# The second MLP of an attention-and-two-MLPs kernel: five pairs of 436-column halves in place of four pairs of 512 and a plain state block

## The chip, the cores and the metric

The kernel runs on one core of one Trainium2 chip. The metric is device time in microseconds (us) of that core, from launch to end, as the median of several runs. The core has a matrix engine (TensorE, PE in the profile, with its weight loads shown apart as PEld), two elementwise engines that matter here (VectorE, DVE, and ScalarE, ACT), and a queue processor (SyncE, SP) that issues every DMA of this kernel in one order.

## The reference, cut to what matters

```python
def _attn_ref(x, state):                      # x (8, 8, 512, 64), state (8, 8, 32, 64)
    scores = scale * np.matmul(x, state.transpose(0, 1, 3, 2))      # softmax over the 32 states
    ...
    xread = np.matmul(a, state)
    ...
    sread = np.matmul(a2, x)
    return np.concatenate([xread, sread], axis=2)

def _moe_ref(x, w_in, w_out):                 # x (4352, 512), w_in (512, 2048), w_out (2048, 512)
    h = x @ w_in
    r = np.maximum(h, 0.0)
    return (r * r) @ w_out

def _moe2_ref(x, w_in, w_out):                # the second MLP: ELU in place of the squared ReLU
    h = x @ w_in
    g = np.where(h > 0.0, h, alpha * (np.exp(np.minimum(h, 0.0)) - 1.0))
    return g @ w_out
```

Each of the 8 batches gives 512 token rows and 32 state rows, so both MLPs see 8 x 544 = 4352 rows. Everything is float32 in effect: a product is made from a high and a low part of each operand in three passes (`product`, lines 41 to 45), low x high, high x high and high x low.

## The kernel before

The data lie transposed, with features on the 128 partitions and tokens along the columns, so a matmul moves up to 512 token columns past a 128x128 block of weights.

**First MLP** (to about 655 us). Attention, the conversion of the 64-bit weights, the first MLP on the eight batches of 512 columns, and at its end the first MLP on the 256 state columns (8 x 32). The conversion also writes, for later, the sums of weight quarters that the second MLP needs (`sums`, `put_split`: DRAM tiles `f_w2..` and `f_v2..`, seven forms of 256 columns with a high and a low part, 2 KB a row and form) and the plain weights `d_w2..`, `d_v2..`. What the first MLP computes is stored into the DRAM tiles `x2d`, one for each batch and one for the state rows.

**Second MLP** (from about 655 us to the end). Four pairs of batches. A pair is one block product of 2x2 blocks by a scheme with seven products in place of eight (Strassen's, in a variant): `x_forms` makes the seven token operands `xf` from two `x2d` tiles (`xr`), `first_product` does seven products for each of eight column blocks of weights (loop `i`, order 1, 7, 2, 5, 4, 3, 6, where 7, 4 and 3 belong to the block before), and `second_product` seven phases of eight blocks (`out_products`: phases 1, 2, 6, 5, 7, 4, 3). Each product of the first is six matmuls of 512 columns, each block of a phase of the second is six too: 2 x 7 x 8 x 6 = 672 matmuls a pair. The weights are streamed: one DMA of 256 KB for each six matmuls (`weight`, tile `wr`, 12 buffers). ACT and DVE make the ELU (`elu`), copy partial sums out of PSUM (`copied`), and split operands into high and low (`split`: ACT the high part, DVE the low). The pair that comes next has its `xr` tiles loaded in the third iteration of `first_product` (`later`), and its operands made during `second_product`.

**State block** (from 1266 us). The 256 state columns go through the second MLP by the plain product, eight blocks of 24 matmuls for `w2` and eight of 24 for `v2`, 384 of 256 columns (`state_block`, with `prepare_s`, `load_plain`, `split_plain`), with plain weights loaded again and split on the fly.

The order of every engine is fixed when the program is built, by a scheduler that goes by its own cost estimates; each engine then works its list from the front. All DMAs wait on SP in one list.

Of the kernel before, what the change touches and what calls it, by code (L numbers as in the profile page):

```python
# [29 lines left out]
NF = 7  # L30
# [6 lines left out]
IN_SINGLE = 13  # L37

# [9 lines left out]
def out_products(nc, split, g, weight, unit, put, sbuf, psum):  # L48
# [6 lines left out]
    def phase(f, src, ps, start, combine=None):  # L55
        for j in range(HF):
            jj, r = divmod(j, 2)
            if combine and r == 0:
                combine(jj)
            if r % unit == 0:  # L60
                t = gp_p.tile([P, 2, unit, S], F32R, name="gp", tag="gp")
                split(t[:, HI], t[:, LO], src[jj][:, r:r + unit])
            w = weight(j, f)
            for m in range(2):
                sl = slice(m * P, (m + 1) * P)
                product(nc, ps[m], [(w[:, HI, sl], w[:, LO, sl])], [(t[:, HI, r % unit], t[:, LO, r % unit])],
                        j == HF - 1, start and j == 0)
            yield next(count)

    def copied(ps, p, name):  # L70
        t = p.tile([P, S], F32, name=name, tag=name)
        act(out=t, in_=ps, func=AF.Copy)
        return t

    def added(e, half, ps, u):
        for m in range(2):
            o = oo_p.tile([P, S], F32, name="o", tag="o")
# [7 lines left out]
    def banks(n):  # L85
        return [psum[n].tile([P, S], F32, name="xyz"[n], tag="xyz"[n]) for _ in range(2)]
# [15 lines left out]
    for m in range(2):  # L102
        o = oo_p.tile([P, S], F32, name="o", tag="o")
# [7 lines left out]
def attn_mlp_kernel(ctx: ExitStack, tc: tile.TileContext, xt, xn, st, w1, v1, w2, v2, outx, outs):  # L111
# [67 lines left out]
    x2d = [dram.tile([P, KC, S if b < B else NST], F32, name=f"x2d{b}", tag=f"x2d{b}") for b in range(B + 1)]  # L179

    if True:
# [77 lines left out]
        wd, wf = {}, {}  # L259

        def sums(v):
# [3 lines left out]
            nc.vector.tensor_tensor(out=t[:, 1], in0=b12, in1=b11, op=ALU.subtract)  # L265
            nc.vector.tensor_tensor(out=t[:, 3], in0=b22, in1=b12, op=ALU.subtract)
            yield t
            nc.vector.tensor_tensor(out=t[:, 2], in0=b22, in1=t[:, 1], op=ALU.subtract)
            nc.vector.tensor_tensor(out=t[:, 0], in0=b21, in1=t[:, 2], op=ALU.subtract)

        def put_split(w, srcs):

            first = 0
            for n, src in srcs:
# [5 lines left out]
                nc.sync.dma_start(out=w[:, first:first + n], in_=h.bitcast(F32))  # L280
                first += n

        def conv_pair(name, j):
# [7 lines left out]
            d = wd[name, j] = dram.tile([P, 2, 512], F32, name=f"d_{name}{j}", tag=f"d_{name}{j}")  # L291
            for r in range(2):
                nc.sync.dma_start(out=d[:, r], in_=v[r])
            for t in sums(v):
                yield
            w = wf[name, j] = dram.tile([P, NF, 2, 256], F32, name=f"f_{name}{j}", tag=f"f_{name}{j}")
            yield from put_split(w, ((1, v[0][:, :256].unsqueeze(1)), (2, v[1].rearrange("p (q f) -> p q f", q=2)),
                                     (2, t[:, :2]), (2, t[:, 2:])))

        def sums_v1(j):  # L300
# [11 lines left out]
            yield from put_split(w, ((2, t[:, :2]), (2, t[:, 2:])))  # L312
# [192 lines left out]
        def out_step():  # L505
# [11 lines left out]
            for k in range(KC):  # L517
# [5 lines left out]
                nc.sync.dma_start(out=x2d[b][:, k], in_=o)  # L523
# [120 lines left out]
        def weight1(j, f):  # L644
            t = wr1_p.tile([P, 2, 256], F32R, name="wr", tag="wr")
            src = {1: lambda: v1d[j][:, :, :256], 2: lambda: v1d[j + HF][:, :, :256],
                   3: lambda: v1d[j + HF][:, :, 256:]}.get(f, lambda: wf["v1", j][:, f - 4])()
# [3 lines left out]
        def pair(b0, bg, order):  # L651
# [27 lines left out]
            def put(e, k, o):  # L679
                nc.sync.dma_start(out=x2d[b0 + e][:, k], in_=o)  # L680
# [94 lines left out]
        def load_xr(b):  # L775
            xr[b] = xr_p.tile([P, KC, S], F32, name=f"xr{b}", tag="xr")
            nc.sync.dma_start(out=xr[b], in_=x2d[b])

        def x_forms(n):
# [4 lines left out]
            def put(f, src):  # L784
                t = xf[n, f] = form_tile(f"xf{n}_{f}", 0)
# [61 lines left out]
        for k in range(KC):  # L847
# [5 lines left out]
            nc.sync.dma_start(out=x2d[B][:, k], in_=o)  # L853
# [7 lines left out]
    wr_p = pool("wr", 12)  # L861
# [8 lines left out]
    def elu(h, out):  # L870

        r = eu_p.tile(list(out.shape), F32, name="r", tag="eu")
# [4 lines left out]
    def copied(ps, p=None, name="eu"):  # L877
        t = (p or eu_p).tile([P, S], F32, name=name, tag=name)
        act(out=t, in_=ps, func=AF.Copy)  # L879
        return t  # L880

    streamed = []

    def weight(name, j, f):
        t = wr_p.tile([P, 2, 256], F32R, name="wr", tag="wr")
        streamed[:] = [nc.sync.dma_start(out=t.bitcast(F32), in_=wf[name, j][:, f - 1])]
        return t

    def first_product(n, g, later):


# [4 lines left out]
        def prod(f, ps, j, start):  # L896
            w, x = weight("w2", j, f), xf[n, f]
# [6 lines left out]
        for i in range(HF + 1):  # L904
# [4 lines left out]
            if i < HF:  # L909
                if i % 2 == 0:  # L910
                    for q in (11, 22, 21, 12):
                        g[q].append(gq_p.tile([P, 2, S], F32, name=f"g{q}", tag="gq"))
                X[i] = ps_x.tile([P, S], F32, name="X", tag="x")
# [5 lines left out]
            if i < HF:  # L919
                y = ps_y.tile([P, S], F32, name="Y", tag="y")  # L920
# [4 lines left out]
                Z[i] = ps_z.tile([P, S], F32, name="Z", tag="z")  # L925
# [18 lines left out]
    def second_product(n, g, bg):  # L944
        def put(e, k, o):
            nc.sync.dma_start(out=outx[k * P:(k + 1) * P, (2 * n + e) * S:(2 * n + e + 1) * S], in_=o)

        for i in out_products(nc, split, g, lambda j, f: weight("v2", j, f), 2, put, (gp_p, eu_p, u2_p, oo_p),
                              (ps_x, ps_y, ps_z)):
# [3 lines left out]

    plain = {}

    def load_plain(name, j):
        t = plain[name, j] = xf_p.tile([P, 2, 512], F32, name="pr", tag="xf")
        nc.sync.dma_start(out=t, in_=wd[name, j])

    def split_plain(name, j):  # L960
        t = form_tile("pl", 80)
        split(t[:, HI], t[:, LO], plain[name, j])
        plain[name, j] = t

    order = [(name, j) for j in range(HF + 2) for name, j in (("w2", j), ("v2", j - 2)) if 0 <= j < HF]
    xs = {}

    def prepare_s():

        raw = xr_p.tile([P, KC, NST], F32, name="xsr", tag="xr")  # L970
        nc.sync.dma_start(out=raw, in_=x2d[B])
        for i in range(2):
            load_plain(*order[i])
        yield
        xs[0] = xr_p.tile([P, 2, KC, NST], F32R, name="xs", tag="xr")
        split(xs[0][:, HI], xs[0][:, LO], raw)
        yield
        for i in range(4):
            split_plain(*order[i])
            if i + 2 < len(order):  # L980
                load_plain(*order[i + 2])
            yield

    def state_block(prepared):
        for _ in prepared:
            pass
        nxt = iter(order[4:])
        ahead = iter(order[6:])

        def refill():  # L990
            x = next(nxt, None)
            if x:
                split_plain(*x)
            x = next(ahead, None)
            if x:
                load_plain(*x)

        gs, acc = {}, []
        for i in range(HF + 2):
            if i < HF:  # L1000
                w = plain.pop(("w2", i))
                ps = ps_x.tile([P, 2, NST], F32, name="hs", tag="x")
                if i == 0:
                    nc.tensor.matmul(ps[:, 0, :P], ident, ident, start=True, stop=True, skip_group_check=True)
                for r in range(2):
                    for d in range(2):
# [86 lines left out]
```

## Time and profile before

| what | value |
|---|---|
| median of 3 runs | 1316.24 us (1314.99 to 1316.87) |
| span of the profiled execution | 1314.0 us |
| TensorE busy | 1302.9 us, 99% of the span, 7020 matmuls |
| DVE busy, ACT busy | 952.7 us (73%), 845.4 us (64%) |
| DMA moved | 305.40 MB, mean 232 GB/s |
| granted TensorE clock | 1.000 of full speed |

The profile is of one execution. Its span goes from the first to the last instruction; the time of a run holds some more at either end, here 2.2 us if the median is set against the span.

### The profile page before, as it was taken

How to read it: one execution, taken by the hardware profiler on the slowest of the kernel's cores; microseconds unless marked ns; L12 is line 12 of the kernel's file. 1: busy time of each engine (PE TensorE's matmuls, PEld its weight loads, DVE VectorE, ACT ScalarE, POOL GpSimd, SP SyncE). 2: the span in 40 equal slices, each digit the busy share in tenths (PEclk: the TensorE clock that was granted, in tenths of full speed). 3: DMA queues.
4: the chain of work that ended last, by engine and by line, in shares of the span. 5: the costliest groups of instructions: out<-in, count | busy, mean ns of one | idle time of the engine just before them, and what ended most of it. 6: DMA issues, size and time to landing. Idle time of an engine off the chain costs nothing.

```text
span 1314.0 us, 19733 instructions
## 1 busy us (share of the span) xinstructions
PE 1302.9 (99%) x7020; PEld 1042.5 (79%) x7020; DVE 952.7 (73%) x1431; ACT 845.4 (64%) x1429; POOL 0.7 (0%) x6
## 2 busy tenths in 40 slices
PE   8999999999999999999999999999999999999999
PEld 6677777777677777778988888888888888888888
DVE  6997878687869955895766963789546984568644
ACT  5997777787765667665567744675446743666444
POOL 0000000000000000000000000000000000000000
PEclk9999999999999999999999999999999999999999
DMA  7999987886734663589697678767786777778733
GB/s 264 321 326 360 336 310 255 294 299 241 266 107 140 203 196 112 166 285 316 207 316 193 196 210 256 237 192 210 215 282 191 209 208 230 204 207 288 220 115 113
DMA packets 138865, 305.40 MB, mean 232 GB/s; under 512 B 14736, under 2 KB 29072, under 8 KB 135696
## 3 DMA queue, kind: packets, MB, share of 16 engines
q1 hardware_dynamic: 138768, 304.15, 72.0%
q8 instruction: 56, 0.92, 0.3%
q14 instruction: 41, 0.34, 0.1%
HBM read 227.54 MB, written 76.55 MB: 231 GB/s over the span
## 4 chain that ended last, share of the span: by engine, by line
PE 83%; DVE 5%; ACT 3%; DMA 3%; issue 1%; SPq 0%; ACTq 0%; DVEq 0%
PE x L44 18%; PE X L44 13%; PE z L44 9%; PE Z L44 6%; PE acc L170 4%; PE acc L172 4%; PE acc L171 4%; PE h L170 4%; PE h L172 4%; PE h L171 4%; PE y L44 3%; PE Y L44 3%; PE mp L349 2%; PE as L44 2%; PE hs L44 1%; DVE g L82 1%
## 5 line engine op out<-in xcount | busy, mean ns | idle before, releaser
L176 DVE TENSOR_TENSOR gp<-g,gp 128x512 fp32r<-128x512 f32 (+1 forms) x224 | 212.4, 955 | 110.9 <-ACT gp L175 109.9
L175 ACT ACTIVATE gp<-g 128x512 fp32r<-128x512 f32 (+1 forms) x224 | 187.4, 843 | 149.8 <-PE x L44 73.8
L44 PE MATMUL x<-gp,wr 128*128 128x512 f32 x1152 | 273.6, 391 | 1.2 <-DVE gp L176 1.1
L44 PEld LDWEIGHTS x<-gp,wr 128*128 128x128 f32 x1152 | 214.8, 188 | 52.9 <-DVE gp L176 4.1
L44 PE MATMUL X<-xf,wr 128*128 128x512 f32 x768 | 186.9, 390 | 0.1
L44 PEld LDWEIGHTS X<-xf,wr 128*128 128x128 f32 x768 | 143.4, 188 | 32.1 <-ACT u L879 1.7
L44 PE MATMUL z<-gp,wr 128*128 128x512 f32 x576 | 133.5, 390 | 0.0
L44 PEld LDWEIGHTS z<-gp,wr 128*128 128x128 f32 x576 | 108.0, 188 | 23.5 <-issue 0.8
L875 DVE SCALAR_TENSOR_TENSOR g<-r,g 128x512 f32<-128x512 f32 x96 | 63.9, 689 | 64.7 <-ACT r L874 64.6
L170 PE MATMUL acc<-gs,v 128*128 128x512 f32 x256 | 103.1, 403 | 0.1
L170 PE MATMUL h<-at,m 128*128 128x512 f32 x256 | 101.6, 397 | 0.8 <-ACT m L175 0.5
L172 PE MATMUL acc<-gs,v 128*128 128x512 f32 x256 | 100.3, 392 | 0.0
L171 PE MATMUL acc<-gs,v 128*128 128x512 f32 x256 | 100.0, 391 | 0.0
L171 PE MATMUL h<-at,m 128*128 128x512 f32 x256 | 99.9, 390 | 0.0
L172 PE MATMUL h<-at,m 128*128 128x512 f32 x256 | 99.9, 391 | 0.0
L44 PE MATMUL Z<-xf,wr 128*128 128x512 f32 x384 | 97.4, 389 | 0.0
L873 ACT ACTIVATE r<-g 128x512 f32<-128x512 f32 x96 | 57.5, 625 | 59.6 <-DVE g L923 42.8
L82 DVE TENSOR_TENSOR g<-g,g 128x1024 f32<-128x1024 f32 x72 | 87.5, 1221 | 0.7
L44 PEld LDWEIGHTS Z<-xf,wr 128*128 128x128 f32 x384 | 72.1, 188 | 15.0
L874 ACT ACTIVATE r<-r 128x512 f32<-128x512 f32 x136 | 81.5, 621 | 0.7
L170 PEld LDWEIGHTS acc<-gs,v 128*128 128x128 f32 x256 | 48.0, 188 | 26.6 <-issue 9.2
L44 PE MATMUL y<-gp,wr 128*128 128x512 f32 x288 | 68.6, 389 | 0.0
(148 smaller groups left out, 2039.4 us busy)
## 6 DMA issues: line engine op xcount, KB each, us to landing
wr<-f_v SPq DMA_DIRECT2D x288, 256.0 KB, 3.1
wr<-f_w SPq DMA_DIRECT2D x224, 256.0 KB, 3.0
f_v<-wf SPq DMA_DIRECT2D x40, 512.0 KB, 4.0
raw_w<-in_w_dram SPq DMA_DIRECT2D x32, 512.0 KB, 5.2
raw_v<-in_v_dram SPq DMA_DIRECT2D x32, 512.0 KB, 5.5
f_w<-wf SPq DMA_DIRECT2D x24, 512.0 KB, 3.7
wr<-p_v SPq DMA_DIRECT2D x48, 256.0 KB, 3.9
xt<-in_xt_dram SPq DMA_DIRECT2D x8, 1024.0 KB, 6.6
```

Of the source, the lines that this page charges most:

```text
L44: nc.tensor.matmul(ps, wk[a], xk[b], start=start and k == 0 and i == 0, stop=last and k == len(w) - 1 and i == 2, skip_group_check=True)
L82: return lambda jj: tt(out=out[jj], in0=a[jj], in1=b[jj], op=ALU.subtract)
L170: mm(ps, w[HI], x[LO], start=first, stop=False)
L171: mm(ps, w[HI], x[HI], start=False, stop=False)
L172: mm(ps, w[LO], x[HI], start=False, stop=last)
L175: copy = nc.scalar.activation(out=hi, in_=src, func=AF.Copy)
L176: nc.vector.tensor_tensor(out=lo, in0=src, in1=hi.bitcast(F32), op=ALU.subtract)
L349: mm(ps[e][32 * k:32 * k + 32, :], st_t[b][r, k, :], x(k, r), start=True, stop=True)
L873: act(out=r, in_=h, func=AF.Relu, scale=-1.0)
L874: act(out=r, in_=r, func=AF.Exp, scale=-1.0)
L875: nc.vector.scalar_tensor_tensor(out=out, in0=r, scalar=-1.0, in1=h, op0=ALU.add, op1=ALU.max)
```

## The change

The second MLP takes all 4352 rows as ten halves (eight of 436 columns, two of 432), that is five pairs, all by the seven-product scheme. The state block with its loads, splits and plain matmuls is gone, and so are the plain weights `d_w2`, `d_v2` that were written for it. `x2d` has a tile for each half now, and `store_x` cuts what the first MLP gives at the halves' borders, so that a store of 512 columns becomes two or three. All tiles of the second MLP are allocated as before and used to 436 (or 432) columns. The seven forms lie in another order in DRAM, so that two of them that are used close to each other are neighbours (`w2`), or two blocks of one form are (`v2`); a weight DMA brings 4 KB a row where it can, into 6 buffers of twice the size. The two outputs become one.

```diff
+TOK = B * ROW
+WIDE = [436, 436, 436, 436, 432]
+ENDS = [sum(w for w in WIDE[:h // 2]) * 2 + (h % 2) * WIDE[h // 2] for h in range(2 * len(WIDE))] + [TOK]
+SLOT = {1: 0, 2: 1, 5: 2, 6: 3, 7: 4, 4: 5, 3: 6}
...
-    x2d = [dram.tile([P, KC, S if b < B else NST], F32, name=f"x2d{b}", tag=f"x2d{b}") for b in range(B + 1)]
+    x2d = [dram.tile([P, KC, WIDE[h // 2]], F32, name=f"x2d{h}", tag=f"x2d{h}") for h in range(2 * len(WIDE))]
+
+    def store_x(b, k, o):
+
+        first, end = b * S, b * S + (S if b < B else NST)
+        for h, at in enumerate(ENDS[:-1]):
+            lo, hi = max(first, at), min(end, ENDS[h + 1])
+            if lo < hi:
+                nc.sync.dma_start(out=x2d[h][:, k, lo - at:hi - at], in_=o[:, lo - first:hi - first])
...
+        wfv = dram.tile([P, NF, HF, 2, 256], F32, name="f_v2", tag="f_v2")
...
-            d = wd[name, j] = dram.tile([P, 2, 512], F32, name=f"d_{name}{j}", tag=f"d_{name}{j}")
-            for r in range(2):
-                nc.sync.dma_start(out=d[:, r], in_=v[r])
             for t in sums(v):
                 yield
-            w = wf[name, j] = dram.tile([P, NF, 2, 256], F32, name=f"f_{name}{j}", tag=f"f_{name}{j}")
-            yield from put_split(w, ((1, v[0][:, :256].unsqueeze(1)), (2, v[1].rearrange("p (q f) -> p q f", q=2)),
-                                     (2, t[:, :2]), (2, t[:, 2:])))
+            if name == "w2":
+                w = wf[name, j] = dram.tile([P, NF, 2, 256], F32, name=f"f_{name}{j}", tag=f"f_{name}{j}")
+            else:
+                w = wfv[:, :, j]
+            yield from put_split(((w[:, 0:1], v[0][:, :256].unsqueeze(1)),
+                                  (w[:, 1:7:5], v[1].rearrange("p (q f) -> p q f", q=2)),
+                                  (w[:, 2:6:3], t[:, :2]), (w[:, 3:5], t[:, 2:])))
...
-        def load_xr(b):
-            xr[b] = xr_p.tile([P, KC, S], F32, name=f"xr{b}", tag="xr")
-            nc.sync.dma_start(out=xr[b], in_=x2d[b])
+        def load_xr(h):
+            xr[h] = xr_p.tile([P, KC, S], F32, name=f"xr{h}", tag="xr")[:, :, :WIDE[h // 2]]
+            nc.sync.dma_start(out=xr[h], in_=x2d[h])
...
-    wr_p = pool("wr", 12)
+    wr_p = pool("wr", 6)
...
-    def weight(name, j, f):
-        t = wr_p.tile([P, 2, 256], F32R, name="wr", tag="wr")
-        streamed[:] = [nc.sync.dma_start(out=t.bitcast(F32), in_=wf[name, j][:, f - 1])]
-        return t
+    def stream(src):
+        t = wr_p.tile([P, 2, 2, 256], F32R, name="wr", tag="wr")
+        t = t[:, :src.shape[1]]
+        streamed[:] = [nc.sync.dma_start(out=t.bitcast(F32), in_=src)]
+        return t
+
+    kept = {}
+
+    def weight1(j, f):
+
+        if (j, f) not in kept:
+            at, fs = next((at, fs) for at, fs in ((0, (1, 2)), (2, (5, 6)), (4, (7,)), (5, (4, 3))) if f in fs)
+            t = stream(wf["w2", j][:, at:at + len(fs)])
+            kept.update({(j, q): t[:, r] for r, q in enumerate(fs)})
+        return kept.pop((j, f))
+
+    def weight2(j, f):
+
+        if (j, f) not in kept:
+            t = stream(wfv[:, SLOT[f], j:j + 2])
+            kept.update({(j + r, f): t[:, r] for r in range(2)})
+        return kept.pop((j, f))
...
-    for n in range(B // 2):
...
-        bg = x_forms(n + 1) if n + 1 < B // 2 else prepare_s()
-        second_product(n, g, bg)
...
-    state_block(bg)
+    for n in range(len(WIDE)):
+        g, more = {}, n + 1 < len(WIDE)
+        first_product(n, g, (lambda: [load_xr(h) for h in (2 * n + 2, 2 * n + 3)]) if more else None)
+        bg = x_forms(n + 1) if more else iter(())
+        second_product(n, g, bg)
+        for _ in bg:
+            pass
```

TensorE's list up to the end of the first MLP is the same in both programs. At the end of the program, before the change, the last phase of the fourth pair (`z`) is followed by the state block (`hs` is the product with `w2`, `as` the one with `v2`):

```order
L44 MATMUL x<-gp,wr 128x512 x48
L44 MATMUL z<-gp,wr 128x512 x48
L44 MATMUL hs<-xs,pl 128x256 x77
L44 MATMUL as<-gss,pl 128x256 x24
L44 MATMUL hs<-xs,pl 128x256 x19
L44 MATMUL as<-gss,pl 128x256 x24
```

With the change TensorE's list ends with the seven phases of the fifth pair:

```order
L48 MATMUL x<-gp,wr 128x432 x40
L48 MATMUL y<-gp,wr 128x432 x48
L48 MATMUL x<-gp,wr 128x432 x48
L48 MATMUL z<-gp,wr 128x432 x48
L48 MATMUL x<-gp,wr 128x432 x96
L48 MATMUL z<-gp,wr 128x432 x48
```

The state block is gone, and the program ends with `z`, whose last sums and stores are what is left to do after the last matmul.

SP's list in `first_product` of the second pair, where the next pair's `xr` tiles are loaded, before (a tile `f_w` with its number is one block of weights with its seven forms, here blocks 1, 2 and 3):

```order
L946 DMA out_dram<-o 128x512 x2
L886 DMA wr<-f_w_1981 128x512
L886 DMA wr<-f_w_2214 128x512 x2
L886 DMA wr<-f_w_1981 128x512 x2
L886 DMA wr<-f_w_2214 128x512
L777 DMA xr_8730<-x2d_142 128x2048
L777 DMA xr_8732<-x2d_143 128x2048
L886 DMA wr<-f_w_2319 128x512
```

And with the change (2215 is block 2, 2317 is block 3):

```order
L979 DMA out_dram<-o 128x436 x2
L895 DMA wr<-f_w_2215 128x1024
L895 DMA wr<-f_w_1981 128x512
L895 DMA wr<-f_w_2215 128x1024
L895 DMA wr<-f_w_1981 128x1024
L790 DMA xr_8592<-x2d_142 128x4x436
L790 DMA xr_8594<-x2d_143 128x4x436
L895 DMA wr<-f_w_2317 128x1024
```

The place among the weights is the same, behind what the third iteration needs of block 2 and before block 3, but a weight DMA carries two units of 512 columns (only form 7 goes alone), and half as many of them can be ahead.

DVE's list at the same place, where it first uses an `xr` tile (`g11` to `g22` are the four quarters of the ELU's result, `gp` the split operand of the second product), before:

```order
L875 SCALAR_TENSOR_TENSOR g22_8510<-r_8602,g22_8510 128x512
L176 TENSOR_TENSOR gp_9207<-g11_8509,gp_9207 128x1024
L875 SCALAR_TENSOR_TENSOR g21_8511<-r_8614,X_8513 128x512
L935 TENSOR_TENSOR g12_8512<-Z_8538,u2_8555 128x512
L792 TENSOR_TENSOR xr5_8732<-xr5_8732 128x1024
L875 SCALAR_TENSOR_TENSOR g12_8512<-r_8627,g12_8512 128x512
```

And with the change:

```order
L968 TENSOR_TENSOR g12_8390<-Z_8414,u2_8429 128x436
L888 SCALAR_TENSOR_TENSOR g12_8390<-r_8497,g12_8390 128x436
L962 TENSOR_TENSOR g22_8388<-Z_8464,eu_8532 128x436
L956 TENSOR_TENSOR g11_8509<-Y_8534,eu_8522 128x436
L805 TENSOR_TENSOR xr5_8594<-xr5_8594 128x2x436
L888 SCALAR_TENSOR_TENSOR g11_8509<-r_8542,g11_8509 128x436
```

The addition on `xr` now stands three rows later, behind the first sum of block 2.

## Rows read from the trace of the kernel before

**Rows 1.** Page: the span, and each engine's busy time, share and instructions.
```profile
span 1314.0 us, 19733 instructions
PE 1302.9 (99%) x7020; PEld 1042.5 (79%) x7020; DVE 952.7 (73%) x1431; ACT 845.4 (64%) x1429; POOL 0.7 (0%) x6
```
**Rows 2.** Chain that ended last, second MLP: start us, us, engine, tile, line, count.
```profile
734.12 7.93 PE x L44 x35
...
887.01 7.93 PE x L44 x35
...
894.94 10.88 PE y L44 x48
...
1040.33 7.93 PE x L44 x35
...
1283.66 2.72 PE hs L44 x24
1286.38 2.72 PE as L44 x24
```
**Rows 3.** Timeline, TensorE where the second MLP begins, then its last run: start us, us.
```profile
654.48 1.55 PE L44 MATMUL Y<-xf,wr 128*128 128x512 f32 x6
...
1302.54 8.32 PE L44 MATMUL as<-gss,pl 128*128 128x256 f32 x72
```
**Rows 4.** Timeline, the end: start us, us, engine, line, operation, [idle before <-releaser].
```profile
1309.27 2.41 SPq L1035 DMA_DIRECT2D out_dram<-o  x4
...
1310.90 0.42 DVE L1032 COPY o<-as 128x256 f32<-128x256 f32 x1 [0.94 <-PE as L44]
```
**Rows 5.** Waits of TensorE's weight loads from 657 us on: total us, times, longest us.
```profile
PEld X L44 <- ACT u L879: 1.7, 5, 0.6
PEld x L44 <- ACT eu L72: 1.4, 4, 0.4
PEld X L44 <- ACT eu L879: 1.0, 5, 0.2
```
**Rows 6.** Groups by shape, 811.7 to 1040 us: busy us, mean ns of one, idle before.
```profile
L176 DVE TENSOR_TENSOR gp<-g,gp 128x1024 fp32r<-128x1024 f32 x31 | 37.9, 1224 | 21.9 <-ACT gp L175 21.7
L175 ACT ACTIVATE gp<-g 128x1024 fp32r<-128x1024 f32 x31 | 32.8, 1057 | 28.5 <-PE x L44 16.0 <-PE z L44 7.3 <-PE y L44 4.0
L929 DVE TENSOR_TENSOR g<-Z,eu 128x512 f32<-128x512 f32 x16 | 11.0, 687 | 7.6 <-ACT eu L879 7.6
L879 ACT ACTIVATE u<-X 128x512 f32<-128x512 f32 x16 | 9.5, 595 | 4.7 <-PE X L44 4.7
```
**Rows 7.** Busy time by stretch: stretch, length, PE, PEld, DVE, ACT, POOL, clock, DMA share, GB/s.
```profile
0.00:430.00 430.00, 423.40 (x2634) 312.67 (x2635) 346.24 (x653) 323.92 (x600) 0.70 (x6) 1.00 0.78 271
430.00:600.00 170.00, 168.85 (x881) 129.59 (x880) 129.98 (x207) 109.80 (x195) 0.00 (x0) 1.00 0.62 197
...
811.00:887.00 76.00, 76.00 (x336) 62.57 (x335) 53.50 (x70) 54.91 (x93) 0.00 (x0) 1.00 0.75 226
887.00:964.00 77.00, 76.99 (x341) 63.40 (x340) 51.28 (x49) 34.29 (x39) 0.00 (x0) 1.00 0.75 216
```
**Rows 8.** Timeline of the third pair's first product at its xr load: start us, us.
```profile
966.00 0.60 ACT L879 ACTIVATE u<-X 128x512 f32<-128x512 f32 x1 [0.63 <-PE X L44]
...
969.08 1.21 SPq L777 DMA_DIRECT2D xr<-x2d  x2
...
978.64 1.23 DVE L792 TENSOR_TENSOR xr<-xr 128x1024 f32<-128x1024 f32 x1 [1.75 <-DMA xr<-x2d]
```
**Rows 9.** Page, DMA issues: count, KB each, median us from issue to landing.
```profile
wr<-f_v SPq DMA_DIRECT2D x288, 256.0 KB, 3.1
xr<-x2d SPq DMA_DIRECT2D x8, 1024.0 KB, 8.4
out_dram<-o SPq DMA_DIRECT2D x32, 256.0 KB, 3.2
x2d<-o SPq DMA_DIRECT2D x24, 256.0 KB, 4.0
d_w<-cv SPq DMA_DIRECT2D x16, 256.0 KB, 6.1
out_dram<-o SPq DMA_DIRECT2D x4, 128.0 KB, 1.7
```
**Rows 10.** Line L886, the weight DMAs of the second MLP: count: ns min/median/max, then landing.
```profile
L886 SPq DMA_DIRECT2D wr<-f_v x224: 319/320/1196, 716.0 to 1250.3; - x112
...
DMA to landing us min/median/max: 2.6/3.0/10.4
```
**Rows 11.** Page: what the DMA engines moved, in 40 equal slices of the span.
```profile
GB/s 264 321 326 360 336 310 255 294 299 241 266 107 140 203 196 112 166 285 316 207 316 193 196 210 256 237 192 210 215 282 191 209 208 230 204 207 288 220 115 113
```

More of the change, by code (lines that the diff above doesn't have):

```diff
@@ L85, in banks @@
     def banks(n):
-        return [psum[n].tile([P, S], F32, name="xyz"[n], tag="xyz"[n]) for _ in range(2)]
+        return [psum[n].tile([P, S], F32, name="xyz"[n], tag="xyz"[n])[:, :n_tok] for _ in range(2)]
     x = banks(0)
@@ L279, in put_split @@
                 nc.vector.tensor_tensor(out=h[:, :, LO], in0=src, in1=h[:, :, HI].bitcast(F32), op=ALU.subtract)
[L280 to L281 removed]
+                nc.sync.dma_start(out=w, in_=h.bitcast(F32))
         def conv_pair(name, j):
@@ L522, in out_step @@
                     nc.scalar.activation(out=o, in_=acc[k], func=AF.Copy)
-                nc.sync.dma_start(out=x2d[b][:, k], in_=o)
+                store_x(b, k, o)
         load_x(0)
@@ L679, in put @@
             def put(e, k, o):
-                nc.sync.dma_start(out=x2d[b0 + e][:, k], in_=o)
+                store_x(b0 + e, k, o)
             def products():
@@ L852, in attn_mlp_kernel @@
                 nc.scalar.activation(out=o, in_=acc[k], func=AF.Copy)
-            nc.sync.dma_start(out=x2d[B][:, k], in_=o)
+            store_x(B, k, o)
         rows.close()
@@ L870, in elu @@
     def elu(h, out):
-        r = eu_p.tile(list(out.shape), F32, name="r", tag="eu")
+        r = eu_p.tile([P, S], F32, name="r", tag="eu")[:, :out.shape[1]]
         act(out=r, in_=h, func=AF.Relu, scale=-1.0)
@@ L945, in put @@
         def put(e, k, o):
-            nc.sync.dma_start(out=outx[k * P:(k + 1) * P, (2 * n + e) * S:(2 * n + e + 1) * S], in_=o)
-        for i in out_products(nc, split, g, lambda j, f: weight("v2", j, f), 2, put, (gp_p, eu_p, u2_p, oo_p),
-                              (ps_x, ps_y, ps_z)):
+            nc.sync.dma_start(out=outx[k * P:(k + 1) * P, ENDS[2 * n + e]:ENDS[2 * n + e + 1]], in_=o)
+        for i in out_products(nc, split, g, weight2, 2, put, (gp_p, eu_p, u2_p, oo_p), (ps_x, ps_y, ps_z), WIDE[n]):
@@ L950, in second_product @@
             if i % HF == 3:
                 next(bg, None)
[L954 to L982, printed above, removed]
@@ L1090 @@
     r = _run(nc, [arrays], core_ids=[0])
-    rows_x, rows_s = (r.results[0][f"out_{i}_dram"].T.reshape(B, -1, DM) for i in range(2))
+    out = r.results[0]["out_0_dram"].T
+    rows_x, rows_s = (t.reshape(B, -1, DM) for t in (out[:B * S], out[B * S:]))
     return _np.concatenate([rows_x, rows_s], axis=1).reshape(B * ROW, DM)
```

112 lines of the change are left out of this document (27 added, 85 removed).

## The prediction

> **What bounds the kernel now.** I read the page first: TensorE is busy for 1302.9 of 1314.0 us [rows 1], so the question is what its matmuls take and where it waits. The chain that ended last answers both for the second MLP [rows 2]. It is one row of matmuls after another, and hardly anything else. A phase of 48 matmuls of 512 columns takes 10.88 us, 226.7 ns for one. A run of 24 matmuls of 256 columns in the state block takes 2.72 us, 113.3 ns for one. That is exactly half: a column costs 0.4427 ns at either width, and a matmul has no fixed part that shows. The reader is to see also how little is lost: the first phase `x` of three successive pairs stands at 734.12, 887.01 and 1040.33 us, so a pair takes 152.89 or 153.32 us, where its 672 matmuls take 672 x 226.7 = 152.32. A pair loses 0.6 to 1.0 us.
>
> The timeline gives the whole [rows 3]: the first matmul of the second MLP starts at 654.48 us, the last run ends at 1302.54 + 8.32 = 1310.86, together 656.38 us. Its matmuls account for 2688 x 226.7 + 384 x 113.3 = 609.3 + 43.5 = 652.8 us, so 3.6 us are lost in all: four pairs at 0.7 and 0.8 in the state block and at the ends. After the last matmul come a copy of 0.42 us and the last store, and the span ends 3.1 us behind the last matmul [rows 4]. The waits of TensorE's weight loads are short and few: 1.7, 1.4 and 1.0 us in total over 14 places [rows 5], all for copies that ACT makes out of PSUM.
>
> So whatever changes the number of columns changes the time in full, and whatever changes the work of DVE, ACT or the DMA queue changes nothing until one of them makes TensorE wait.
>
> **The change, part by part.**
>
> *Columns.* The plain product of the state rows needs eight products where the scheme needs seven. Before: 2688 x 512 + 384 x 256 = 1,474,560 columns. After: four pairs of 672 matmuls with 436 columns and one of 672 with 432, that is 2688 x 436 + 672 x 432 = 1,462,272. At 0.4427 ns a matmul of 436 takes 193.0 ns and one of 432 takes 191.3, together 518.8 + 128.5 = 647.4 us in place of 652.8: **5.4 us less**. There are 288 matmuls more, and that is free only because the rows show no fixed part.
>
> Here a rule of the Trainium skill says something else (TensorE: Matmul & The Clock Gate, "Back-to-back issue gap"): warm, a matmul takes its columns at 2.4 GHz plus about 2.5 ns. By that, a page's figure and not this trace's, 512, 256, 436 and 432 columns would take 215.8, 109.2, 184.2 and 182.5 ns, and the saving would be 622.1 - 617.7 = 4.4 us. The two widths of this trace disagree with it, since 226.7 is twice 113.3 with nothing left over, so I keep 5.4.
>
> *Lost time.* Five pairs at 0.7 us are 3.5, in place of 3.6. I take it as unchanged. What could raise it is that ACT and DVE shrink less than TensorE. From 1024 to 512 columns a DVE operation falls from 1224 to 687 ns, 1.05 ns a column and 150 fixed; at 436 it takes 607 ns, and 872 columns take 1065, that is 0.87 to 0.88 of before. ACT goes from 595 at 512 (slope to 1057 at 1024: 0.90 ns) to 527, 0.885 of before [rows 6]. TensorE's step, six matmuls, shrinks to 0.852 (1.360 to 1.158 us). Over the pair from 811 to 964 us DVE was busy 53.5 + 51.3 = 104.8 of 153 us, 68%, and ACT 89.2, 58% [rows 7]; that becomes about 71 and 60%. Neither is a bound, but the margins inside a step get narrower (first rival).
>
> *The load of the next operands.* It was issued at 969.08 us, DVE came to the addition on it 1.75 us before 978.64, that is 7.8 us later, and waited 1.75 us; DVE's list waits with it [rows 8]. The load now goes out behind the second weight tile of block 1. With six buffers that tile is issued when the buffer of block 1's first tile comes free, after the seventh step of the pair; DVE comes to the addition behind the sum of block 2's second product, after the fourteenth. That is some 7.5 steps, 7.5 x 1.158 = 8.7 us, against a landing of 8.4 us for loads that are 1.17 times as large [rows 9]. So it should wait less than before, and I count nothing. The bounds: 0.4 us a pair gained (what the second of the two pairs above lost more than the first), or the same lost.
>
> *The weights.* Half as many DMAs of twice the size, in 4 KB rows. The list lets a weight tile go out nine steps before it is needed in the first product (block 3's first tile takes the buffer that step 9 frees, and is used in step 18, counted from 0), 10.4 us, and about ten in the second. Half-size loads landed in 3.0 us at the median and 10.4 at the most [rows 10]. Both products need 256 KB a step, 226 GB/s in place of 193, so the DMA engines go from 221 to some 255 GB/s; at the same price a byte their share rises from 0.75 to 0.87. They reached 336 and 360 GB/s in slices of the first MLP [rows 11], so I count nothing; the upper bound is in the second rival. The larger rows gain nothing either, since no row of [rows 5] waits for a weight.
>
> *The first MLP.* TensorE's list is the same. The plain weights' 32 stores go (6.1 us of landing each for those of `w2` [rows 9]), and 36 more stores of `x2d` come (72 pieces for 36); SP spends 0.32 us on an issue [rows 10], so its list is 1.3 us longer in all, spread over eight places. TensorE lost 6.6 us up to 430 us and 1.2 us up to 600 [rows 7]; I see no reason for a sign. Zero, with 1.5 us either way.
>
> *The end.* The last store was 128 KB and landed in 1.7 us; now the last sums are additions of 432 columns (0.60 us for 0.42) and a store of 216 KB, between 1.7 and the 3.2 us that 256 KB took beside the weights' traffic [rows 4, 9]. I take 0.2 + 0.6 = **0.8 us more**, bounds 0.2 and 1.7.
>
> **The sum.** 1314.0 - 5.4 + 0.8 = 1309.4 us of span. The median of the three runs, 1316.24, lies 2.2 us above the profiled span; with the same 2.2 us the time is **1311.6 us**, 0.35% less. A difference of less than 0.2%, 2.6 us, is about what a measurement of this kernel cannot tell from no change; the forecast is 2 us beyond that border.
>
> **The rivals.**
>
> 1. *Copies come late in the first product.* Between a block's product 6 and its product 7, on the same PSUM tile, stands one other product; in that time ACT must have copied the tile. The cover falls from 1.360 to 1.158 us, the copy from 0.60 to 0.53, so the margin shrinks by 0.13 us. For it: this wait is the longest of those that there are. Against it: it came up 5 times in 32 blocks, and in most places ACT was idle before the copy (0.63 us in one such row [rows 8]). If each of 40 blocks lost 0.13 us more, that is 5.2 us: 1316.8, no change.
>
> 2. *A weight comes late, and the kernel gets slower.* The weights of the first product have 10.4 us now where twelve small buffers gave eleven steps of 1.36, 15 us. The place is the third iteration, where 1.7 MB of operands go out just ahead of block 3's weights. It decides from the point at which a weight lands more than 10.4 us behind its issue, which is the longest of before [rows 10]. If the engines are fuller by a seventh, the longest may be 12.4: 2 us in each of four pairs, 8 us: 1319.6, slower.
>
> 3. *Columns are handled in larger lots.* The rows have widths of 512 and 256 only, both multiples of 64. If 436 and 432 each cost as much as 448, a matmul takes 198.3 ns and the second MLP 666.4 us without its losses, 13.6 us more than before: 1330.6, slower. Nothing in the rows speaks for it but that no other width stands there.
>
> 4. *The first MLP ends later.* If SP's longer list at the end of each batch holds up conversions or loads as the 1.2 us up to 600 us did, 2 to 4 us are lost: 1313.6 to 1315.6, no change.
>
> **How the numbers follow.** Forecast 0.68, the first rival 0.13, the second 0.09, the third 0.05, the fourth 0.05. Faster by over 0.2% is below 1313.6, slower above 1318.9: the forecast lies in the first, the first and the fourth rival between, the second and the third in the last; faster 0.68, same 0.18, slower 0.14. The low end: 0.8 for the end becomes 0.2, the first MLP gives 1.5 us, the loads of operands 0.4 in four pairs: 1311.6 - 0.6 - 1.5 - 1.6, about 1308. The high end takes in the first and the fourth rival and the second up to its price: 1319.5.
>
> **What the profile after would show.** A phase of 48 matmuls at 9.27 us (9.18 in the last pair) shows the columns right; 9.52 shows the third rival. A pair of 130.4 us from one first `x` to the next shows the lost time right. The second MLP's first matmul at 654.5 us shows that the first MLP stood still. Waits of TensorE for copies above some 8 us in all are the first rival, any for `wr` the second. The last matmul should end near 1305.5 and the span 3.9 us behind it. What would make the prediction wrong is any wait that repeats in each of the 40 blocks: 0.1 us there is 4 us.

## The result: slower, outside the forecast's range

| | median of the runs, us | lowest to highest |
|---|---|---|
| before (4 runs) | 1315.62 | 1314.19 to 1316.87 |
| after (4 runs) | 1325.64 | 1323.69 to 1326.69 |

The ratio is 1.0068, with an interval of 1.0053 to 1.0083: the change makes the kernel 0.7% slower. The forecast was 1311.6 us, and 1319.5 at most.

The page of the kernel after answers [rows 1]:

```profile
span 1321.9 us, 20162 instructions
PE 1311.2 (99%) x7306; PEld 1125.0 (85%) x7306; DVE 958.6 (73%) x1513; ACT 849.7 (64%) x1517; POOL 0.7 (0%) x6
```

The span has grown by 7.9 us and TensorE's busy time by 8.3: nothing new waits, the matmuls themselves take longer. The chain that ended last shows where (it answers [rows 2]; start us, us, engine, tile, line, count):

```profile
723.96 6.73 PE x L48 x34
730.69 9.49 PE y L48 x48
...
857.28 6.72 PE x L48 x34
...
902.01 9.55 PE x L48 x48
911.56 9.28 PE z L48 x48
...
995.63 9.49 PE y L48 x48
...
1261.57 9.40 PE y L48 x48
...
1308.88 9.41 PE z L48 x48
```

A phase of 48 matmuls of 436 columns takes 9.49 us, 197.8 ns for one, in place of the 9.27 that were forecast; one of 432 columns takes 9.40, 195.8 ns, in place of 9.18. A single stretch keeps to the forecast: the phase at 911.56 with its 9.28 us, 193.3 ns for one. It belongs to some 415 matmuls from 902 to 983 us; the other 2273 of 436 columns take 197.8. From 723.96 to 857.28 a pair takes 133.3 us, where 130.4 were forecast.

The rest stands as it was. The second MLP begins at 654.14 us, where it began at 654.48 [rows 3] and the end looks like [rows 4] (timeline; start us, us, [idle before <-releaser]):

```profile
654.14 1.16 PE L48 MATMUL Y<-xf,wr 128*128 128x436 f32 x5
...
1317.72 1.21 DVE L82 TENSOR_TENSOR o<-z,u 128x432 f32<-128x432 f32 x2 [4.45 <-PE z L48]
1318.35 0.93 SPq L979 DMA_DIRECT2D out_dram<-o  x2
```

The last matmul ends at about 1318.1 us and the span 3.8 us behind it. The waits of TensorE's weight loads from 657 us on answer [rows 5], and of DVE's waits one is for the operands (total us, times, longest us):

```profile
PEld x L48 <- ACT eu L76: 2.0, 5, 0.4
PEld X L48 <- ACT u L922: 1.4, 7, 0.2
PEld X L48 <- ACT eu L922: 0.6, 3, 0.2
...
DVE xr L805 <- DMA xr<-x2d: 2.5, 3, 0.9
```

They are as short as before, and none is for a weight, although a weight DMA now takes 4.2 or 4.3 us to land (page, DMA issues: count, KB each, median us):

```profile
wr<-f_v SPq DMA_DIRECT2D x140, 512.0 KB, 4.2
wr<-f_w SPq DMA_DIRECT2D x120, 512.0 KB, 4.3
```

### The profile page after: what moved, and what is told of

Read it like the earlier page. It is cut to its first block, busy times and chain, and to the rows that moved or that the text cites. A ratio compares the mean times of both kernels' runs of the same rounds, so it can differ in the third digit from the quotient of the medians.

```text
span 1321.9 us, 20162 instructions
## 1 busy us (share of the span) xinstructions
PE 1311.2 (99%) x7306; PEld 1125.0 (85%) x7306; DVE 958.6 (73%) x1513; ACT 849.7 (64%) x1517; POOL 0.7 (0%) x6
## 4 chain that ended last, share of the span: by engine, by line
PE 88%; DVE 4%; ACT 4%; issue 1%; DMA 1%; ACTq 0%; SPq 0%; DVEq 0%
PE x L48 21%; PE X L48 14%; PE z L48 10%; PE Z L48 7%; PE acc L174 4%; PE y L48 4%; PE acc L176 4%; PE acc L175 4%; PE h L174 4%; PE h L175 4%; PE h L176 4%; PE Y L48 4%; PE mp L362 2%; DVE g L86 1%; DVE gp L180 1%
## 5 line engine op out<-in xcount | busy, mean ns | idle before, releaser
L180 DVE TENSOR_TENSOR gp<-g,gp 128x512 fp32r<-128x512 f32 (+2 forms) x252 | 224.6, 896 | 121.6 <-ACT gp L179 120.2
L179 ACT ACTIVATE gp<-g 128x512 fp32r<-128x512 f32 (+2 forms) x252 | 199.2, 796 | 165.5 <-PE x L48 81.3
L48 PE MATMUL x<-gp,wr 128*128 128x436 f32 (+2 forms) x1344 | 289.3, 369 | 0.2
L48 PE MATMUL X<-xf,wr 128*128 128x436 f32 (+1 forms) x960 | 204.3, 359 | 0.0
L48 PE MATMUL z<-gp,wr 128*128 128x436 f32 (+2 forms) x672 | 141.9, 368 | 0.6 <-DVE gp L180 0.6
L888 DVE SCALAR_TENSOR_TENSOR g<-r,g 128x436 f32<-128x436 f32 (+1 forms) x120 | 70.6, 609 | 72.4 <-ACT r L887 72.4
L48 PE MATMUL Z<-xf,wr 128*128 128x436 f32 (+1 forms) x480 | 107.5, 358 | 0.0
L886 ACT ACTIVATE r<-g 128x436 f32<-128x436 f32 (+1 forms) x120 | 64.6, 561 | 61.9 <-DVE g L956 44.0
L86 DVE TENSOR_TENSOR g<-g,g 128x872 f32<-128x872 f32 (+2 forms) x84 | 92.5, 1106 | 1.1
L887 ACT ACTIVATE r<-r 128x436 f32<-128x436 f32 (+1 forms) x160 | 85.3, 556 | 0.8
L48 PE MATMUL y<-gp,wr 128*128 128x436 f32 (+2 forms) x336 | 72.6, 368 | 0.0
```

Source lines behind the costliest of these rows:

```text
L48: nc.tensor.matmul(ps, wk[a], xk[b], start=start and k == 0 and i == 0, stop=last and k == len(w) - 1 and i == 2, skip_group_check=True)
L86: return lambda jj: tt(out=out[jj], in0=a[jj], in1=b[jj], op=ALU.subtract)
L179: copy = nc.scalar.activation(out=hi, in_=src, func=AF.Copy)
L180: nc.vector.tensor_tensor(out=lo, in0=src, in1=hi.bitcast(F32), op=ALU.subtract)
L886: act(out=r, in_=h, func=AF.Relu, scale=-1.0)
L887: act(out=r, in_=r, func=AF.Exp, scale=-1.0)
```

## The experiments

Two theories stood against each other at first. **The price of a width**: a matmul of 436 columns takes 197.8 ns whatever else is at work. **The traffic**: something beside it, the 4 KB rows above all, holds each matmul up by 4.5 ns. In what follows, a steady price is the mean distance between the starts of successive matmuls in the trace, in a stretch without waits. TensorE's granted clock was 1.00 in all stretches from which a steady price is taken, its level of 2.4 GHz.

### The columns without the new streaming

```diff
-    wr_p = pool("wr", 6)
+    wr_p = pool("wr", 12)
...
+        return stream(wf["w2", j][:, SLOT[f]])
...
+        return stream(wfv[:, SLOT[f], j])
```

The changed kernel with one DMA of 256 KB for each form and twelve buffers, as before the change; the order of the forms in DRAM stays the new one.

> Five pairs of 436-column halves as in the change, but the weights streamed as before: one DMA of 256 KB for each form and block into 12 small buffers. Theory A (two paces: a matmul of 436 columns takes 193.3 ns or about 4.5 ns more, whatever feeds it, and the program runs mostly at the slower pace): 48 matmuls again in 9.49 us (197.8 ns each), time again near 1325 us. Theory B (the 4 KB rows or the six larger buffers are what slows the matmuls): 9.28 us for 48, time near 1314 us. Theory C (columns in lots of 64): 9.52 us for 48 in both kinds of pairs.

Measured: 1329.4 us (1326.23 to 1331.62), 1.0081 of before (1.0061 to 1.0101). Every phase of 436 columns takes as long as with the new streaming (chain):

```profile
732.10 9.49 PE y L48 x48
...
1267.05 9.40 PE y L48 x48
```

So the 4 KB rows do not make the matmuls longer. Its profiled span is 5.5 us above that of the changed kernel: the second MLP begins 1.5 us later, the stretch at 193.3 ns is missing (415 x 4.5 = 1.9), and the rest is in waits, one of which, for DVE, is of 1.6 us.

### The new streaming without the columns

The kernel before, with the order of the forms in DRAM, the double DMAs and the six buffers of the change; widths of 512 and the state block stay.

```diff
-    def weight(name, j, f):
-        t = wr_p.tile([P, 2, 256], F32R, name="wr", tag="wr")
...
+    def stream(src):
+        t = wr_p.tile([P, 2, 2, 256], F32R, name="wr", tag="wr")
...
-            w, x = weight("w2", j, f), xf[n, f]
+            w, x = weight1(j, f), xf[n, f]
```

> Four pairs of 512-column halves and the state block as before, with only the new weight streaming (4 KB rows, six buffers). Theory A: 512 columns stay at 226.7 ns (10.88 us for 48), time that of the kernel before within 3 us. Theory B: about 231 ns (11.1 us for 48), time 10 us or more above before. Theory C says nothing here: no change.

Measured: 1318.03 us (1314.73 to 1319.51), 0.9998 of before (0.9985 to 1.0011). The chain has the old prices:

```profile
743.89 10.88 PE y L45 x48
...
1268.00 5.67 PE hs L45 x48
```

The streaming shows neither a cost nor a gain. The loss comes with the columns.

### Other widths in the whole kernel

Four kernels differ from the changed one in one line, the widths of the five pairs:

```diff
-WIDE = [436, 436, 436, 436, 432]
+WIDE = [448, 448, 448, 448, 384]
+WIDE = [512, 480, 464, 416, 304]
+WIDE = [512, 512, 512, 384, 256]
+WIDE = [512, 512, 512, 320, 320]
```

> The change with halves of 448 columns in four pairs and 384 in the fifth, the same number of columns in all. Theory A: 198.3 or 202.8 ns at 448, 170.0 or 174.5 at 384; if the slower pace holds mostly, near 1325 us again. Theory C (lots of 64): 198.3 and 170.0 ns only, that is 647.4 us of matmuls and a time near 1312 us. If widths that are multiples of 64 keep the faster pace by themselves, the time is also near 1312.

> The change with five widths in one program: halves of 512, 480, 464, 416 and 304 columns, the same total. Theory A: faster pace 226.7, 212.5, 205.4, 184.2, 134.6 ns, slower pace about 4.5 ns above each, the extra being the same at every width; 512 stays at the faster. Theory C: 226.7, 226.7, 226.7, 198.3, 141.7 ns, a time above 1340 us.

> The change with three pairs of 512-column halves, one of 384 and one of 256, the same total. Theory R: 226.7 at 512 with nothing extra, 173.3 at 384, 113.3 or 117.8 at 256: matmuls 649.6 to 652.6 us and time 1311 to 1316 us, if the elementwise engines keep up at 256. Rival (extra of about 4.5 ns at every matmul of the changed program): 15 us of extras, 1325 us.

> The change with three pairs of 512-column halves and two of 320 (the name is a leftover). Theory R: nothing extra at 512, 3 to 4.5 ns at 320: 457.0 + 1344 x 144.7 to 146.2 = 651.4 to 653.4 us of matmuls, time 1314 to 1318 us. Rival (4.5 ns at every matmul): 1325 us.

Measured: 1324.22 us for the first, 1.0046 of before (1.0027 to 1.0064); 1322.27 us for the second, one run; 1325.6 for the third, 1.0063 (1.0046 to 1.0081); 1320.0 for the fourth, 1.0018 (1.0002 to 1.0035). Their chains show the price of each width, here two phases of 448 columns (first kernel), one of 256 (third) and one of 320 (fourth):

```profile
731.90 9.73 PE y L48 x48
...
868.71 9.92 PE y L48 x48
```

```profile
1279.52 5.76 PE y L48 x48
```

```profile
1171.94 7.04 PE y L48 x48
```

By its share of 226.7 ns, 448 columns would take 198.3; they take 202.7 or 206.7 (9.73 and 9.92 us for 48), so a width that is a multiple of 64 does not escape, and the third rival falls. The second kernel ran 480, 464, 416 and 304 columns at 216.7, 208.9, 188.4 and 137.8 ns, 4.2, 3.5, 4.2 and 3.2 above their shares, so it is not one extra for all widths either. The last two kernels came out above what was expected (1311 to 1316 us and 1314 to 1318). 256 columns, at 113.3 ns in most of the state block of before, take 119.8 in a pair, 4.4 us more for 672 matmuls, and there TensorE also waited, some 4 us of it for weights; 320 columns take 146.7. No choice of widths beat the kernel before; the fourth comes nearest.

### Bare matmuls of 23 widths

To take all other work away, the kernel before got matmuls behind its last store: on fixed tiles, four runs of 48 for each width, and between two runs one copy by ACT. (This kernel and the three after it with bare matmuls took 2141.68, 2148.88, 1936.93 and 2609.5 us; only their prices are of use.)

```diff
+        for n in LIST:
+            for rep in range(4):
+                for i in range(48):
+                    nc.tensor.matmul(ps[:, :n], t[:, i % 2, 1, :P], t[:, i // 2 % 2, 0, :n], start=True, stop=True,
+                                     skip_group_check=True)
+                act(out=e[:, :n], in_=ps[:, :n], func=AF.Copy)
```

> The kernel before, and behind its last store runs of 48 matmuls on fixed tiles, four runs for each of 23 widths from 512 to 128 columns, with a copy by ScalarE between runs, while no DMA and no other engine works. Theory D (the extra 4.5 ns come from other traffic, DMA or elementwise engines on the same memory): 436 and 432 columns take 193.3 and 191.3 ns in all four runs. Theory W (a weight load that is not quite hidden): an extra at every width alike, 512 included. Theory R (a matmul's length must fit a raster that the engine keeps, so the extra depends on the width and on where the run starts): 512 and 256 at 226.7 and 113.3 ns after at most some 24 matmuls, 436 at 193.3 or 197.8, 432 near 195.8, 464 near 209 or 210, 480 near 216.7, 416 near 188.3, 384 near 173.3.

Some of the runs in the timeline (start us, us, [idle before]):

```profile
1326.31 11.17 PE L1051 MATMUL pm<-tm 128*128 128x512 f32 x48 [0.75 <-ACT em L1053]
...
1551.91 9.77 PE L1051 MATMUL pm<-tm 128*128 128x436 f32 x48 [0.68 <-ACT em L1053]
...
1763.65 8.92 PE L1051 MATMUL pm<-tm 128*128 128x400 f32 x48 [0.65 <-ACT em L1053]
...
1938.38 7.32 PE L1051 MATMUL pm<-tm 128*128 128x320 f32 x48 [0.59 <-ACT em L1053]
...
2053.02 6.01 PE L1051 MATMUL pm<-tm 128*128 128x256 f32 x48 [0.53 <-ACT em L1053]
```

A run stands some 0.3 us above 48 times its steady price, for its first matmuls and its tail: 436 columns have 9.77 us here and 9.49 in the middle of the kernel. The steady prices of the last 24 matmuls, ns, and what they hold above columns / 2.4:

| columns | steady ns | above | columns | steady ns | above |
|---|---|---|---|---|---|
| 512 | 226.67 | 13.33 | 400 | 180.00 | 13.33 |
| 480 | 216.67 | 16.67 | 384 | 173.33 | 13.33 |
| 464 | 208.9, 210.0 | 15.6, 16.7 | 352 | 160.00, 161.1 | 13.33, 14.5 |
| 448 | 202.7 | 16.0 | 320 | 146.67 | 13.33 |
| 436 | 197.8 | 16.1 | 304 | 137.8 | 11.1 |
| 432 | 195.83 | 15.83 | 256 | 120.0 | 13.33 |
| 424 | 190.0, 193.33 | 13.3, 16.7 | 192 | 111.67 | 31.67 |
| 416 | 188.33 | 15.00 | 128 | 111.67 | 58.33 |

This is the answer to the main question. With nothing else at work, 436 columns take what they take in the kernel, so the traffic falls. And a matmul has a fixed part: 512, 400, 384, 352, 320 and 256 columns take their columns at 2.4 GHz and 13.33 ns more (352 in three of its four runs), other widths of 240 columns and more 11 to 17. Below some 240 columns (112.0 ns) the price no longer falls. The prices of theory R, most of them already seen in the kernels above, came out but for 256 columns: 120.0 in place of 113.3.

### Smaller weights, and two-byte operands

The same runs with weight blocks of 64 and of 32 columns, and then with bf16 operands and full blocks, to see whether the extra comes from the weight load or from the operands' size.

```diff
+        for x, c, ns in ((t, 64, WIDE64), (t, 32, WIDE64), (tb, P, WIDEB)):
...
+                        nc.tensor.matmul(ps[:c, :n], x[:, i % 2, 1, :c], x[:, i // 2 % 2, 0, :n], start=True,
+                                         stop=True, skip_group_check=True)
```

> As the run of bare widths, with weight blocks of 64 and of 32 columns in place of 128, and then with bfloat16 tiles and full weights. Theory W (the weight load): with 64 columns of weights the extra of 436 and 432 falls from 4.5 to about half or to nothing, with 32 to nothing. Theory R (raster of the moving columns): the same extras as with 128 columns of weights; in bfloat16 no forecast, if the 17 for 16 belongs to four-byte columns then 512 takes less than 226.7 ns.

```profile
1436.13 9.66 PE L1056 MATMUL pm<-tm 128*64 128x436 f32 x48 [0.68 <-ACT em L1058]
...
1701.26 9.76 PE L1056 MATMUL pm<-tm 128*32 128x436 f32 x48 [0.67 <-ACT em L1058]
...
1970.66 9.00 PE L1056 MATMUL pm<-tb 128*128 128x436 bf16 x48 [0.68 <-ACT em L1058]
```

A block of a half or a quarter of the weights leaves 436 columns at 196.7 and 200.0 ns, so the extra is not in proportion to the weight load. 512 columns even take more, 230.0 and 231.7, while 432 fell to 191.1 in two of four runs and in one of four. So neither theory came out: the extra does not go with the weights, and it is not the same as with full blocks. Every matmul in these runs has a weight load of its own, so what matmuls on weights that stay would take was not tested. With bf16, 512, 436, 256 and 128 columns take 215.83, 184.17, 109.17 and 55.83 ns: each is columns / 2.4 and 2.50 ns more. The large and uneven fixed part belongs to the four-byte operands.

### What sets the pace of 436 columns

Why did some 415 matmuls run at 193.3? The next run has 436 columns behind breaks of 18 lengths, behind one matmul of another width, and at other places in the tile, then widths near 436, then 480 matmuls in a row.

```diff
+LIST = ([(436, 0, 0, k, 48) for k in range(24, 437, 24)] + [(436, a, 0, 436, 48) for a in range(32, 513, 32)]
+        + [(436, 0, o, 436, 48) for o in (4, 8, 16, 32, 64, 72)] + [(n, 0, 0, 436, 48) for n in (440, 440, 444, 444, 428, 428, 420, 420, 404, 404)]
+        + [(436, 0, 0, 436, 480)])
```

> The kernel before with bare runs behind its last store, on fixed tiles and with no other work: 16-odd runs of 48 matmuls of 436 columns behind breaks of different length (the copy between two runs takes 24 to 432 columns), 16 behind one matmul of another width, 6 with the moving operand 4 to 72 columns into its tile, then widths 440, 444, 428, 420, 404, and one run of 480 matmuls of 436. If the pace of a run is set by where the first matmul falls in a raster, the runs of 436 show both paces, 197.8 and 193.3 ns, by their break or their lead, and one can be chosen; if by the address, the runs with an offset differ. If the pace of 193.3 in the changed kernel came from something else (its tiles, the traffic), all runs show 197.8 ns. By a fixed part of 13.3 ns, which 512, 400, 384, 368, 352, 336 and 320 columns showed, 440, 444, 428, 420 and 404 would take 196.7, 198.3, 191.7, 188.3 and 181.7 ns; I expect 1 to 5 ns more for these, as for 436.

```profile
1330.61 9.77 PE L1055 MATMUL pm<-tm 128*128 128x436 f32 x48 [0.34 <-ACT em L1057]
1340.74 9.55 PE L1055 MATMUL pm<-tm 128*128 128x436 f32 x48 [0.36 <-ACT em L1057]
1350.67 9.77 PE L1055 MATMUL pm<-tm 128*128 128x436 f32 x48 [0.38 <-ACT em L1057]
1360.84 9.55 PE L1055 MATMUL pm<-tm 128*128 128x436 f32 x48 [0.40 <-ACT em L1057]
...
1838.49 95.21 PE L1055 MATMUL pm<-tm 128*128 128x436 f32 x480 [0.69 <-ACT em L1057]
```

Every 20 ns of break turns the pace: all runs of this first group alternate between 197.8 (9.77 us) and 193.3 ns (9.55). It is the length and not the order: behind breaks of one length, all four runs of 436 columns among the 23 widths kept 197.8. A run then keeps its pace, the last one over all 480 matmuls ((95.21 - 0.28) / 480 = 197.8). Of the 16 leads one, 416 columns, gave 193.3. Another place in the tile, tried behind one length of break, moved the price between 197.3 and 200.0 and never to 193.3. 440, 444 and 428 took 200.0, 200.0 and 196.0; 420 took 186.67 in one run and 193.33 in the other, 404 took 182.2 and 183.3; one run of 420 lies 1.7 ns below what a fixed part of 13.3 gives, where 1 to 5 more were expected. So a pace is set when a stretch begins, by the length of the break before it or the matmul that leads it; the data's address moves the price a little. That a raster inside the engine lies behind it is not shown.

The last bare run asks whether a single matmul between can turn the pace with no break: four times 24 of 436 columns with one of another width in between, for 32 widths.

```diff
+                n = w if i % 25 == 24 else 436
```

> The kernel before with 64 bare chains behind its last store: each four times 24 matmuls of 436 columns with one matmul of another width (16 to 512 columns in steps of 16, each width twice, behind breaks of two lengths) between the 24s and no break inside. If the pace is a matter of where a matmul starts in a raster, an odd matmul between can move a chain from 197.8 to 193.3 ns and back, by its width; if only a break sets it, all four 24s of a chain keep one pace. A width that leads to 193.3 ns from either pace would give a version of the changed kernel that is some 13 us faster.

Measured (ns a matmul, the mean of the last twelve distances in each of a chain's four 24s; the two chains of a width):

| width between | first chain | second chain |
|---|---|---|
| 16 | 193.3, 197.8, 197.8, 197.8 | 193.3, 197.8, 197.8, 197.8 |
| 336 | 197.8, 193.3, 197.8, 197.8 | 197.8, 193.3, 197.8, 197.8 |
| 496 | 197.8, 193.3, 193.3, 193.3 | 197.8, 193.3, 193.3, 193.3 |
| 512 | 197.8, 193.3, 193.3, 193.3 | 197.8, 197.8, 197.8, 197.8 |

A single matmul can turn it, both ways. Ones of up to 240 columns always led to 197.8; in 12 of the 64 chains, all with 256 columns or more between, a 24 behind the first ran at 193.3. 496 columns led to 193.3 and kept it in both of their chains.

### Useless matmuls that steer the kernel

With that, ten or twenty matmuls of 496 columns were added to the changed kernel, whose result is overwritten:

```diff
+def odd(nc, ps, w):
+
+    nc.tensor.matmul(ps[:, :ODD], w[:, HI, :P], w.rearrange("p a b -> p (a b)")[:, :ODD], start=True, stop=True,
+                     skip_group_check=True)
...
+            if f in AT_PHASE and j == 0 and n_tok < S:
+                odd(nc, full[id(ps)], w)
```

> The changed kernel with ten useless matmuls of 496 columns more, two in each pair: ahead of the second block's Y in the first product and ahead of phase y in the second, into a PSUM tile that is written anew behind it. By the theory that the extra time is a pace that is set by where a matmul starts, each of them may move the stretch behind it from 197.8 to 193.3 ns, as a 496-column matmul did in the bare chains, until the next wait sets the pace anew: up to some 500 of a pair's 672 matmuls, 500 x 4.45 ns x 5 = 11 us less, for 10 x 0.22 = 2.2 us more: between 1316.8 (all move) and 1327.8 us (none does), and the stretches behind a useless matmul are seen at 193.3 in the trace. By any theory in which the matmuls are held up by something else, 2.2 us more than the changed kernel's 1325.6 and no stretch changes.

> The same with twenty, four in each pair: also ahead of the fifth block's Y and of phase z. Costs 4.5 us; a stretch that the first of two did not move has a second chance, and one that it moved may fall back. If the moves are certain, no better than with ten (1318 to 1319); if they are a matter of chance for each, about as many stretches at 193.3 as with ten; if none moves, 1330.1.

Measured: 1327.47 us with ten, 1.0071 of before (1.0045 to 1.0098), and 1327.84 with twenty, 1.0070 (1.0045 to 1.0094). With ten, no stretch turned behind one; a single stretch of 252 matmuls ran at 193.3, from a wait at 1120 us on. With twenty, phase `z` turned in three of the four pairs of 436 columns, here the first (chain):

```profile
733.53 9.49 PE y L50 x48
743.02 9.49 PE x L50 x48
752.74 9.28 PE z L50 x48
762.03 9.28 PE x L50 x48
```

Y of the fifth block turned in two of four, and all three stretches that `z` turned outlived the next wait: some 1110 of the 2688 matmuls ran at 193.3. That is 695 more than in the changed kernel, 695 x 4.5 = 3.1 us, for 20 x 0.223 = 4.5 us of useless work, so no gain. But work that was added made the work behind it faster at once. A pace explains that; a hold-up by the traffic does not. The turn is not certain enough to build on, and no kernel here beats the one before.

## Why the prediction was wrong, step by step

**Columns: the step that failed.** It says that "a column costs 0.4427 ns at either width, and a matmul has no fixed part that shows", and that 288 matmuls more are free "only because the rows show no fixed part". The two rows under it do give that line, but neither end means what I took it for. 512 columns are 213.33 ns of columns and 13.33 fixed; 256 columns in most of the state block are 106.67 and 6.67, the best of three paces of that width, which took 120.0 in the bare runs and 119.8 in a pair. That the second fixed part is half the first is a coincidence, and it put the fixed part of the line through the two points at zero. In steps:

| second MLP's matmuls | us |
|---|---|
| before: 2688 x 226.67 + 384 x 113.3 ns | 652.8 |
| after, as forecast | 647.4 |
| after, with 13.33 ns fixed: 2688 x 195.0 + 672 x 193.3 | 654.1 |
| after, as paced: 2273 x 197.8 + 415 x 193.3 + 672 x 195.8 | 661.4 |

The fixed part alone takes the saving back and more (6.7 us), and the uneven paces of 436 and 432 columns add 7.3. The two together are 14.0 us on a forecast of 5.4 less.

The sign stood in the trace of before. The chain there has a row that I did not use, 48 of the state block's first 77 matmuls, of the same 256 columns:

```profile
1266.62 5.67 PE hs L44 x48
```

That is 118.1 ns for one beside the 113.3 of [rows 2]: the same width at two prices, with nothing waiting. (Counted at their price, the first 77 add some 0.3 us to the matmuls of before.) Whoever sees this cannot draw a line through one of them.

**The rule that was set aside.** The Trainium skill (TensorE: Matmul & The Clock Gate, "Back-to-back issue gap") gives a single warm matmul its columns at 2.4 GHz and about 2.5 ns. The bf16 runs agree with it to the hundredth (215.83 ns at 512 columns). I set it aside because it did not fit the two widths, and threw away its form with its figure: at seven widths this kernel's operands have that form, with a fixed part five times as large.

**Lost time: right.** Forecast 3.5 us, counted as the 3.6 of before. From 654.14 to 1318.1 us are 664.0, less 661.4: 2.6 lost. In the trace of before, one more wait than in [rows 5], 0.3 us for DVE's `gss` in the state block, was left out of the count; it changes nothing.

**The load of the next operands: right.** DVE waited 2.5 us for it in three places, 0.9 at most; before it was 2.8 us in three places, 1.8 at most. None of TensorE's waits is for it.

**The weights: right.** Nothing waits for one, and the new streaming alone is 0.9998 of before.

**The first MLP: right.** Its end moved by 0.3 us, inside the 1.5 that were left open.

**The end: right.** 3.8 us behind the last matmul, forecast 3.9.

**The sum again.** 1309.4 of span, with 14.0 more for the columns, less 1.0 lost, less 0.3 for the earlier start and less 0.1 at the end, gives 1322.0; the profiled span is 1321.9.

**The rivals.** The first, second and fourth did not come: no waits for copies beyond those of before, none for weights, no later start. The third, columns in lots of 64, named the right place and even nearly the price (198.3 for 197.8), by a wrong mechanism: 448 columns take 202.7 or 206.7, not 198.3, and it would have made 432 as dear as 436. It had 0.05; with the row of 118.1 ns read, a price of its own for an unseen width deserved far more.

## What to carry to other kernels

A price per column that is read from two widths says nothing of a third: where a change brings a width, or a number of matmuls, that the trace has not got, time that width by itself first. Look for rows in which the same shape has two prices and nothing waits; they say that the price is a pace and not a rate. With four-byte operands and full weight blocks no width here had a lower price per column than the 0.4427 ns of 512 columns, which 256 reached only at the best of their paces, and a product that saves an eighth of the columns of a small block can lose it again in shorter matmuls.

## What the runs showed of the hardware that was not expected

- With four-byte operands a matmul's steady price is columns / 2.4 GHz and 13.33 ns at 512, 400, 384, 368, 352 (three of four runs), 336 and 320 columns; at others of 240 columns and more it is columns / 2.4 GHz and mostly 11 to 17 ns (6.67 at the best pace of 256, 18.3 at the worst of 436 and 420); the bare runs with full weight blocks came down to 111.7 ns at the least (128 and 192 columns). With bf16 it is 2.50 ns at every one of eight widths.
- A width can have several steady paces: 436 columns 193.3, 197.8 and, elsewhere in the tile, 200.0 ns, 448 columns 202.7 and 206.7, 256 columns 113.3, 117.8 and 120.0. Which one holds is set where a stretch begins, can turn with 20 ns of a break or with one matmul of another width, and was kept for 480 matmuls of 436 columns.
- Behind a break, the first dozen four-byte matmuls of 272 columns and more, with full weight blocks, took some 8 to 11 ns more each on average, the first some 100 ns more (303 in place of 193 at 436 columns). This start, other than the steady part, goes with the weight block: with blocks of 64 and 32 columns the first took some 250 and 220 ns beside steady 196.7 and 200.0. bf16 matmuls were at their price from the start.
- What in the chip makes these paces was not shown. Some of the distances fit steps of 6.67 ns (193.33 is 29 of them; three matmuls at 197.8 are 89), but no run here looks inside, and it stays open.
